# Counting the first expert's tokens on two engines with three PSUM banks, and transposing the first softmax one chunk of scores later

## The chip, the cores and the metric

The kernel runs on one core of one Trainium2 chip. Its time is the device time of one execution in microseconds (us). Before the change it is 1360.89 us, the median of three runs (1357.67 to 1362.44). The core has TensorE (PE in the profile; PEld are its weight loads), VectorE (DVE), ScalarE (ACT), GpSimd (POOL) and SyncE (SP), each with a queue of its own that it works off in order, and 16 DMA engines that all queues share.

## The reference

Attention between channels, then a mixture of eight experts. There are 4 batches of 5056 tokens with 256 channels, 20224 tokens in all.

```
qn = q / (norm(q, axis=1) + 1e-6);  kn = k / (norm(k, axis=1) + 1e-6)   # over the tokens
s  = kn^T @ qn / tau            # per batch: 256 x 256
a  = softmax(s)                 # over the last axis
x  = (v @ a)                    # 20224 x 256
logits = x @ w_gate             # 20224 x 8
# go through all (token, expert) pairs by falling logit; a token takes the first expert
# that still has room; each expert takes cap = 20224 / 8 = 2528 tokens
for e in range(8):
    out[mine[e]] = relu(x[mine[e]] @ w1[e]) @ w2[e]    # 256 -> 1024 -> 256
```

## The kernel before, in words

**Scores stage.** For each batch, five chunks of 1024 tokens (the last has 960 in 120 partitions) are loaded by SP as two halves with `k` and `q` side by side in a tile `ua`, of which there are four. TensorE adds `k^T q` into a PSUM bank (L239, 16 fp32 products per chunk); ScalarE squares the halves (L247) and VectorE sums the squares (L248) for the norms. After the fifth chunk four pairs of small products give the norms (L256), and a few operations make the scaling vectors (`lengths`).

The softmax of batch b runs on VectorE while TensorE does the scores of batch b+1: two small products spread the scaling (L281), VectorE makes the matrix `ac` (ending at L311), four transposes turn it (L319, `turned_a`), products with the gate weights follow (L328, `gates`), and ScalarE writes the result as `a` (L330, L331). With `a` a chunk of values can be multiplied (L197, `x_tiles`: 16 products, one value job) and its result `x` stored to DRAM by ScalarE's queue (L207). What stands where is given by tables: `LOADS` (which value chunk is loaded behind which chunk of scores), `JOBS` (which jobs stand behind which chunk: "x" a value job of batch 0, "l" a piece of the logits, L343) and `GATES_AT` (behind which chunk the transposes stand for batches 1 and 2; the gates stand one chunk later). Inside this stage a scheduler orders the instructions of an engine from the order in which they are written.

**Routing.** The thirteen value chunks left over (`TODO`) keep TensorE busy while VectorE routes the first expert. For each expert a search over thresholds (`route`: eight steps, each comparisons on VectorE, 20 products L495 and one L508 on TensorE) finds the expert's tokens. `compact` then turns the mask into an index list: for each of the 20 columns of 128 slots, TensorE multiplies (L704) into a PSUM tile `pi` that holds three columns, ScalarE counts with a sign function that accumulates (L709, one instruction and a read per column), and copies two more numbers out as `ext` (L712). With the counts of all columns VectorE computes the list `src` (L715 to L746). `pi` is one PSUM bank, so the products of the next three columns wait for the `ext` of the three before.

From here on a planner written in the kernel (class `Order`) sets the order: each stream of work names an engine and a cost, and the planner puts it between the main products when its modelled time has come. `compact` is such a stream.

**Experts.** GpSimd gathers an expert's tokens by `src` from DRAM (L937), TensorE transposes them (L964), ScalarE and VectorE split them into a high and a low part (`xH`, `xL`), and two layers follow (L999 with `hH`, `hL` of L1002 and L1007; L1030 with `y`), whose rows GpSimd scatters to the output (L1037). The weights of an expert are gathered by its number (L907) and split into `ua` in eight pieces (L916 on ScalarE, L919 on VectorE). The search for the next expert runs between these products.

## Time and profile before

| | us |
|---|---|
| median of three runs | 1360.89 (1357.67 to 1362.44) |
| profiled execution, its own time | 1353.34 |
| span of its instructions | 1351.6 |
| TensorE busy | 1306.5 (97%) |
| VectorE busy | 758.3 (56%) |
| ScalarE busy | 532.7 (39%) |
| GpSimd busy | 357.2 (26%) |

The scores stage ends near 210 us, the value chunks near 343 us, and the first products of an expert start at 352.4 us. A line of the profile such as `L704 PE MATMUL pi<-E_,G` is line 704 of the kernel, the engine, the operation, and the tiles written and read. In a row of the timeline the first number is the start and the second the time to the end of the last of the merged instructions; the bracket is the engine's idle time before it and what ended it.

### The profile page before, as it was taken

Reading aid. Unit: us, or ns where it says so; the run is one execution under the profiler, and the core shown is the slowest. Engines: PE = TensorE matmul, PEld = TensorE weight load, DVE = VectorE, ACT = ScalarE, POOL = GpSimd, SP = SyncE. Lnnn points to the kernel's source line nnn. Section 1 sums busy time; section 2 is a strip of 40 time slices with the busy share of each in tenths; the row PEclk is TensorE's granted clock in tenths of the full one; section 3 lists DMA queues with packets and bytes.
Section 4 is the critical chain, followed back from the end, with each engine's and each line's share of the span. In section 5 each row is a group of like instructions: output and inputs, shape, how many; then the busy total and the mean of one; then the engine's idle time right before and its main releaser. Section 6 shows DMA issues by size and latency. Waiting matters only on the chain.

```text
span 1351.6 us, 22840 instructions
## 1 busy us (share of the span) xinstructions
PE 1306.5 (97%) x9138; PEld 1154.2 (85%) x9138; DVE 758.3 (56%) x1890; ACT 532.7 (39%) x1210; POOL 357.2 (26%) x526
## 2 busy tenths in 40 slices
PE   8989999999599999999999999999999999999998
PEld 6878877887488888888889888989898998899898
DVE  6746395767478659668657666672334224233321
ACT  5545452236134334435325424344533334333321
POOL 0000010000322443334323423333334333434122
PEclk9989999999699999999999999999999999999999
DMA  8998974245312112112111311131122113111000
GB/s 288 385 345 316 325 237 176 94 136 196 98 31 87 51 59 94 44 44 101 47 33 44 112 33 40 44 104 44 51 70 85 36 48 108 51 44 57 16 32 31
DMA packets 53706, 143.13 MB, mean 106 GB/s; under 512 B 7776, under 2 KB 28640, under 8 KB 48992
## 3 DMA queue, kind: packets, MB, share of 16 engines
q1 hardware_dynamic: 14544, 62.40, 13.4%
q0 software_dynamic: 17664, 58.22, 13.2%
q10 hardware_dynamic: 21392, 21.06, 4.6%
q8 instruction: 71, 1.16, 0.4%
q14 instruction: 35, 0.29, 0.1%
HBM read 99.97 MB, written 41.68 MB: 105 GB/s over the span
## 4 chain that ended last, share of the span: by engine, by line
PE 71%; issue 12%; DVE 5%; POOL 5%; DMA 4%; ACT 1%; another core or an unknown queue 1%; SPq 0%; POOLq 0%; ACTq 0%
PE ph L999 25%; PE py L1030 24%; PE px L197 9%; PE s L239 7%; POOL out_dram L1037 3%; DMA x_d<-xs 2%; PE pc L495 2%; POOL xg L937 2%; DMA ua<-in_q_dram 2%; PE pt L964 1%; PE px L343 1%; PE pi L704 1%; DVE acc_q L248 1%; DVE ge L526 0%
## 5 line engine op out<-in xcount | busy, mean ns | idle before, releaser
L1030 PE MATMUL py<-ua,hH 128*128 128x256 f32 (+1 forms) x2560 | 468.1, 283 | 0.0
L999 PE MATMUL ph<-xH,ua 128*128 128x512 f32 (+3 forms) x1312 | 420.4, 393 | 9.4 <-issue 6.4
L1030 PEld LDWEIGHTS py<-ua,hH 128*128 128x128 f32 (+1 forms) x2560 | 390.3, 186 | 0.4
L1030 PE MATMUL py<-ua,hL 128*128 128x256 f32 (+1 forms) x1280 | 358.4, 280 | 0.0
L1007 DVE SCALAR_TENSOR_TENSOR hL<-ph,hH 128x512 fp32r<-128x512 f32 (+3 forms) x328 | 219.0, 669 | 178.7 <-ACT hH L1002 141.3
L1037 POOL DMA_INDIRECT out_dram<-y,idx x160 | 160.4, 1003 | 545.7 <-ACT y L1035 500.3
L999 PEld LDWEIGHTS ph<-xH,ua 128*128 128x128 f32 x1312 | 245.6, 190 | 59.8 <-issue 6.6
L1002 ACT ACTIVATE hH<-ph 128x512 fp32r<-128x512 f32 (+3 forms) x328 | 190.4, 583 | 247.3 <-PE ph L999 205.9
L999 PE MATMUL ph<-xL,ua 128*128 128x512 f32 (+3 forms) x656 | 256.9, 392 | 0.2 <-DVE xL L969 0.2
L1030 PEld LDWEIGHTS py<-ua,hL 128*128 128x128 f32 (+1 forms) x1280 | 238.6, 186 | 0.0
L1035 ACT ACTIVATE y<-py 128x256 f32<-128x256 f32 (+1 forms) x160 | 61.4, 384 | 337.6 <-PE py L1030 280.0
L937 POOL DMA_INDIRECT xg<-x_d,src x160 | 154.2, 964 | 119.0 <-issue 45.1
L239 PE MATMUL s<-ua 128*128 128x256 f32 (+1 forms) x640 | 146.4, 390 | 7.4 <-DMA ua<-in_q_dram 7.4
L239 PEld LDWEIGHTS s<-ua 128*128 128x128 f32 (+1 forms) x640 | 124.3, 196 | 27.4 <-issue 6.2
L999 PEld LDWEIGHTS ph<-xL,ua 128*128 128x128 f32 x656 | 125.0, 190 | 23.7 <-DVE xL L969 0.8
L969 DVE TENSOR_TENSOR xL<-pt,xH 128x512 fp32r<-128x512 f32 (+3 forms) x82 | 54.5, 665 | 125.6 <-ACT xH L966 125.0
L197 PE MATMUL px<-a,vr 128*128 128x256 f32 (+1 forms) x448 | 103.4, 385 | 0.9 <-ACT a L331 0.9
L247 ACT ACTIVATE sq<-ua 128x1024 f32<-128x1024 f32 (+1 forms) x72 | 75.8, 1056 | 58.4 <-DMA ua<-in_k_dram 24.5
L197 PEld LDWEIGHTS px<-a,vr 128*128 128x128 f32 x448 | 82.9, 190 | 12.3 <-ACT a L331 1.0
L201 ACT ACTIVATE xs<-px 128x512 f32<-128x512 f32 (+1 forms) x96 | 50.2, 527 | 91.5 <-PE px L197 88.0
L709 ACT ACTIVATE junk<-pi,rhalf 128x160 bf16<-128x160 f32 x160 | 61.8, 391 | 33.0 <-PE pi L704 27.2
L498 DVE TENSOR_TENSOR Dm<-pc,dmask 128x64 f32<-128x64 f32 (+3 forms) x63 | 12.7, 201 | 86.8 <-PE pc L495 56.9
(265 smaller groups left out, 1091.6 us busy)
## 6 DMA issues: line engine op xcount, KB each, us to landing
x_d<-xs ACTq DMA_DIRECT2D x19, 1024.0 KB, 4.6
ua<-in_k_dram SPq DMA_DIRECT2D x31, 512.0 KB, 5.9
ua<-in_q_dram SPq DMA_DIRECT2D x31, 512.0 KB, 7.2
vr<-in_vt_dram SPq DMA_DIRECT2D x14, 1024.0 KB, 10.6
ua<-in_vt_dram SPq DMA_DIRECT2D x4, 1024.0 KB, 5.2
ua<-in_k_dram SPq DMA_DIRECT2D x8, 480.0 KB, 6.7
ua<-in_q_dram SPq DMA_DIRECT2D x8, 480.0 KB, 8.8
xg<-x_d,src POOLq DMA_INDIRECT x160
```

The lines of the kernel that those rows point to most:

```text
L197: mm = PE.matmul(px[:, i * C:i * C + width], lhsT=vs[b, c][:, kb, t + i, :], rhs=a_f[b][:, kb, 0:width], start=(kb == 0), stop=(kb == 1))
L239: newest[0] = PE.matmul(sb[:, ib * C:(ib + 1) * C], lhsT=kt[:np_, t, ib * 128:(ib + 1) * 128], rhs=qt[:np_, t, :], start=(first and t == 0 ...
L247: S.activation(sq[:np_], t_[:np_], AF.Square)
L709: S.activation(junk, pi[:, i * W:i * W + COLS], AF.Sign, bias=rhalf[:, g0 + i:g0 + i + 1], scale=-1.0, accum_out=sgn[:, g0 + i:g0 + i + 1])
L937: queue.append(lambda i=i, col=col, n=n_in(col): P.indirect_dma_start(out=xg[:n, i, :], out_offset=None, in_=x_d, in_offset=bass.IndirectO ...
L969: V.tensor_tensor(xL[:, kb, 0:nt], pt[:, 0:nt], xH[:, kb, 0:nt].bitcast(F32), op=OP.subtract)
L999: PE.matmul(ph[:, 0:nt], lhsT=l[:, w], rhs=x_[:, kb, 0:nt], start=(i == 0), stop=(i == 5))
L1002: S.activation(hH[:, fb, 0:nt], ph[:, 0:nt], AF.Relu)
L1007: V.scalar_tensor_tensor(hL[:, fb, 0:nt], ph[:, 0:nt], 0.0, hH[:, fb, 0:nt].bitcast(F32), op0=OP.max, op1=OP.subtract)
L1030: PE.matmul(py[:n, 0:C], lhsT=l[:, fb, tk], rhs=w[:, d], start=(j == 0), stop=(j == 23))
L1035: S.activation(y[:n], py[:n, 0:C], AF.Copy)
L1037: sd = P.indirect_dma_start(out=out, out_offset=bass.IndirectOffsetOnAxis(ap=idx[:n, col:col + 1], axis=0), in_=y[:n], in_offset=None)
```

## The change

1. **The scores stage's tables.** `GATES_AT` puts the first transposes behind the fourth chunk of scores instead of the third, and the gates behind the fifth. The value jobs of batch 0 and the first pieces of the logits each move back one place. The softmax is written behind the jobs of chunk 0 instead of ahead of them.
2. **The first expert's `compact`** is cut into two streams: `by_act` tests the first 11 columns on ScalarE as before, out of two PSUM banks; `by_dve` tests the other 9 on VectorE with a comparison that accumulates, out of the bank that there was. VectorE then turns both counts into `at`. The other seven experts keep the old way. The two new banks come from a pool that is closed when the experts' pools open.
3. **The waits ahead of the experts' pools**: the loop that lets the planner run until the first expert's number and list are there stands before the pools are opened instead of behind.

```diff
+NACT = 11
-JOBS = {(1, 3): [("x", 0)], (1, 4): [("x", 1)], (2, 0): [("x", 2)], (2, 1): [("x", 3)], (2, 2): [("x", 4)],
-        (2, 4): [("l", 0)], (3, 0): [("l", 1)], (3, 1): [("l", 2)],
+JOBS = {(1, 4): [("x", 0)], (2, 0): [("x", 1)], (2, 1): [("x", 2)], (2, 2): [("x", 3)], (2, 3): [("x", 4)],
+        (3, 0): [("l", 0)], (3, 1): [("l", 1)], (3, 2): [("l", 2)],
         "tail": [("w", (1, 1)), ("l", 3), ("l", 4), ("l", 5), ("l", 6), ("l", 7)]}
-GATES_AT = (2, 3)
+GATES_AT = (3, 3)
...
-                put(0, soft)
+                todo[0].append(soft)
...
+    cctx = ExitStack()
+    two = [cctx.enter_context(tc.tile_pool(name="two", bufs=2, space=PSUM))]
...
+        def by_act():
+            todo = list(range(0, NACT, RB))
+            held = []
+            while todo or held:
+                while todo and len(held) < 2:
+                    g0 = todo.pop(0)
+                    n = min(RB, NACT - g0)
+                    pi = two[0].tile([128, 512], F32, name="pi")
+                    yield "P", n * 75
+                    tested(pi, g0, n)
+                    held.append((pi, g0, n))
+                pi, g0, n = held.pop(0)
+                for i in range(n):
+                    yield "A", 700
+                    junk = rtile("junk", dt=BF, bufs=2)
+                    S.activation(junk, pi[:, i * W:i * W + COLS], AF.Sign, bias=rhalf[:, g0 + i:g0 + i + 1], scale=-1.0,
+                                 accum_out=sgn[:, g0 + i:g0 + i + 1])
+                yield "A", 200
+                S.activation(ext[:, g0:g0 + n], pi[:, 0:n * W].rearrange("p (i w) -> p i w", w=W)[:, :, COLS:W], AF.Copy)
...
+        def by_dve():
+            num = rtile("num", (128, NCOL))
+            for g0 in range(NACT, NCOL, RB):
+                n = min(RB, NCOL - g0)
+                pi = ps_c.tile([128, 512], F32, name="pi")
+                yield "P", n * 75
+                tested(pi, g0, n)
+                for i in range(n):
+                    yield "V", 370
+                    junk = rtile("junkv", dt=BF, bufs=2)
+                    V.tensor_scalar(junk, pi[:, i * W:i * W + COLS], rhalf[:, g0 + i:g0 + i + 1], 0.0, op0=OP.is_lt,
+                                    op1=OP.add, accum_out=num[:, g0 + i:g0 + i + 1])
+                yield ve(2 * n, psum=True)
+                V.tensor_copy(ext[:, g0:g0 + n], pi[:, 0:n * W].rearrange("p (i w) -> p i w", w=W)[:, :, COLS:W])
+            yield ve(NCOL)
+            V.tensor_copy(at[:, NACT:NCOL], num[:, NACT:NCOL])
...
+        if p == 0:
+            o.add(by_act(), lambda: COMPACT_PRIO)
+            o.add(by_dve(), lambda: COMPACT_PRIO - 1)
...
+        o.until(("ei", 0))
+        settle()
+        o.until(("idx", 0))
         actx.close()
+        cctx.close()
...
-        o.until(("ei", 0))
-        settle()
-        o.until(("idx", 0))
```

Three places show how instructions move. Line numbers of the changed kernel are its own, a few above those of the profile (L320 is the old L319, L725 and L728 the old L709 and L712). First, TensorE from the first softmax's L281 to the second's; before:

```order
L281 MATMUL pc<-dq,ones_f 128x128 x2
L239 MATMUL s<-ua 128x256 x32
L319 MATMUL pm<-ident,ac 128x128 x4
L239 MATMUL s<-ua 128x256 x16
L328 MATMUL pm<-wg_t,aT 128x8 x4
L197 MATMUL px<-a_169,vr 128x264 x16
L239 MATMUL s<-ua 128x256 x16
L197 MATMUL px<-a_169,vr 128x264 x16
L256 MATMUL pc<-ones_f,acc_k 128x1 x2
L256 MATMUL pc<-ones_f,acc_q 128x1 x2
L239 MATMUL s<-ua 128x256 x16
L281 MATMUL pc<-dq,ones_f 128x128 x2
```

and now:

```order
L282 MATMUL pc<-dq,ones_f 128x128 x2
L240 MATMUL s<-ua 128x256 x48
L320 MATMUL pm<-ident,ac 128x128 x4
L240 MATMUL s<-ua 128x256 x16
L329 MATMUL pm<-wg_t,aT 128x8 x4
L257 MATMUL pc<-ones_f,acc_k 128x1 x2
L257 MATMUL pc<-ones_f,acc_q 128x1 x2
L198 MATMUL px<-a_169,vr 128x264 x16
L240 MATMUL s<-ua 128x256 x16
L198 MATMUL px<-a_169,vr 128x264 x16
L282 MATMUL pc<-dq,ones_f 128x128 x2
```

Three chunks of scores instead of two now stand between L281 and the transposes, and no value job stands before the batch's last chunk any more; from one L281 to the next the amount of work is the same.

Second, ScalarE behind the store of a value chunk (L207, now L208) during the first expert's counting; before:

```order
L207 DMA x_d<-xs 1024x1x256
L712 ACTIVATE ext<-pi 128x6
L201 ACTIVATE xs<-px 128x2x256
L916 ACTIVATE ua<-ub 128x512
L709 ACTIVATE junk,sgn<-pi,rhalf 128x160 x2
L201 ACTIVATE xs<-px 128x2x256
L916 ACTIVATE ua<-ub 128x512
L709 ACTIVATE junk,sgn<-pi,rhalf 128x160
L201 ACTIVATE xs<-px 128x2x256
L916 ACTIVATE ua<-ub 128x512
L712 ACTIVATE ext<-pi 128x6
```

and now:

```order
L208 DMA x_d<-xs 1024x1x256
L725 ACTIVATE junk,sgn<-pi,rhalf 128x160 x2
L202 ACTIVATE xs<-px 128x2x256
L971 ACTIVATE ua<-ub 128x512
L725 ACTIVATE junk,sgn<-pi,rhalf 128x160
L728 ACTIVATE ext<-pi 128x6
L202 ACTIVATE xs<-px 128x2x256
L971 ACTIVATE ua<-ub 128x512
L725 ACTIVATE junk,sgn<-pi,rhalf 128x160 x2
```

Between the store and the next `ext` but one there stood three evictions (L201) and three weight pieces (L916) before; now one of each stands before the second set's `ext`.

Third, VectorE at the same time, with the next expert's first steps (`m`, `t`, `khi`, `eq`) between its tests; now:

```order
L741 TENSOR_SCALAR junkv,num<-pi,rhalf 128x160
L454 TENSOR_REDUCE m<-L_146 128x160
L741 TENSOR_SCALAR junkv,num<-pi,rhalf 128x160
L457 TENSOR_SCALAR t_2230<-m 128x160
L741 TENSOR_SCALAR junkv,num<-pi,rhalf 128x160
L460 TENSOR_SCALAR tie<-t_2230 128x160
L744 COPY ext<-pi 128x6
L462 TENSOR_TENSOR t_2230<-t_2230,tie 128x160
L465 TENSOR_SCALAR khi<-t_2230 128x160
```

All L741 and L744 rows are new on VectorE; the others stood here before in the same order.

More of the change, by code (lines that the diff above doesn't have):

```diff
@@ L698, in compact, with tested @@
         ext = rtile("ext", (128, NCOL, 2))
-        for g0 in range(0, NCOL, RB):
+        at = rtile("at", (128, NCOL), I32)
+        ended = []
+        def tested(pi, g0, n):
+            for i in range(n):
+                PE.matmul(pi[:, i * W:(i + 1) * W], lhsT=G[:, (g0 + i) * 128:(g0 + i + 1) * 128], rhs=E_,
+                          start=True, stop=True)
+        def by_act():
[17 more added lines that the diff above has]
+                S.activation(ext[:, g0:g0 + n], pi[:, 0:n * W].rearrange("p (i w) -> p i w", w=W)[:, :, COLS:W], AF.Copy)
+            ended.append(1)
@@ new lines, in by_dve @@
+        def by_dve():
[5 more added lines that the diff above has]
+                tested(pi, g0, n)
+                for i in range(n):
+                    yield "V", 370
[6 more added lines that the diff above has]
+            V.tensor_copy(at[:, NACT:NCOL], num[:, NACT:NCOL])
+            ended.append(1)
@@ L700, in compact @@
+        if p == 0:
+            o.add(by_act(), lambda: COMPACT_PRIO)
+            o.add(by_dve(), lambda: COMPACT_PRIO - 1)
+            while len(ended) < 2:
+                yield "W", 0
+            yield ve(NCOL)
+            V.tensor_scalar(at[:, 0:NACT], sgn[:, 0:NACT], 0.5, COLS / 2.0, op0=OP.mult, op1=OP.add)
+        for g0 in range(0, NCOL if p else 0, RB):
             n = min(RB, NCOL - g0)
@@ L702, in compact @@
             yield "P", n * 75
+            tested(pi, g0, n)
             for i in range(n):
-                PE.matmul(pi[:, i * W:(i + 1) * W], lhsT=G[:, (g0 + i) * 128:(g0 + i + 1) * 128], rhs=E_,
-                          start=True, stop=True)
-            for i in range(n):
-                yield "A", 600 if p else 900
+                yield "A", 600
                 junk = rtile("junk", dt=BF, bufs=2)
@@ L712, in compact @@
             S.activation(ext[:, g0:g0 + n], pi[:, 0:n * W].rearrange("p (i w) -> p i w", w=W)[:, :, COLS:W], AF.Copy)
-        at = rtile("at", (128, NCOL), I32)
-        yield ve(NCOL)
-        V.tensor_scalar(at, sgn, 0.5, COLS / 2.0, op0=OP.mult, op1=OP.add)
+        if p:
+            yield ve(NCOL)
+            V.tensor_scalar(at, sgn, 0.5, COLS / 2.0, op0=OP.mult, op1=OP.add)
         k1 = rtile("k1", (128, NCOL), I32)
```

## The prediction

> **What bounds the kernel now.** I read the page's busy shares, then TensorE's waits from 0 to 365 us, where the edit lies. The busy line and four of the waits:
>
> ```profile
> PE 1306.5 (97%) x9138; PEld 1154.2 (85%) x9138; DVE 758.3 (56%) x1890; ACT 532.7 (39%) x1210; POOL 357.2 (26%) x526
> PE pm L319 <- DVE ac L311: 4.1, 1, 4.1
> PE pi L704 <- ACT ext L712: 2.6, 2, 2.4
> PE pc L281 <- DVE dq L280: 2.3, 2, 1.5
> PE ph L999 <- issue: 6.4, 1, 6.4
> ```
>
> TensorE is busy in 97% of the span, so only its idle time, its slow time and work taken off it can move the end. (A row of waits gives the sum in us, how often, the longest.) Two of these waits belong to steps that the change touches in the scores stage: 4.1 us for the first softmax's `ac`, 2.3 us for `dq`. The third, 2.6 us for `ext`, belongs to the first expert's counting. The fourth, at the first expert's first products, has no named cause.
>
> TensorE's own timeline over the first wait, batch 1's scores onward (start, duration, instruction, records, wait in brackets; two records to an fp32 product, so x32 is one chunk):
>
> ```profile
> 60.28 7.14 PE L239 MATMUL s<-ua 128*128 128x256 f32 x32 [0.62 <-DMA ua<-in_q_dram]
> 71.57 1.08 PE L319 MATMUL pm<-ident,ac 128*128 128x128 f32 x4 [4.14 <-DVE ac L311]
> 72.44 9.48 PE L239 MATMUL s<-ua 128*128 128x256 f32 x32
> 81.76 0.95 PE L328 MATMUL pm<-wg_t,aT 128*128 128x8 f32 x8
> 83.66 7.39 PE L197 MATMUL px<-a,vr 128*128 128x264 f32 x32 [0.95 <-ACT a L331]
> 90.89 7.07 PE L239 MATMUL s<-ua 120*128 120x256 f32 x32
> 97.80 7.29 PE L197 MATMUL px<-a,vr 128*128 128x264 f32 x32
> 104.92 0.50 PE L256 MATMUL pc<-ones_f,acc_k 128*128 128x1 f32 x4
> 105.73 7.15 PE L239 MATMUL s<-ua 128*128 128x256 f32 x32
> 114.36 0.46 PE L281 MATMUL pc<-dq,ones_f 128*128 128x128 f32 x2 [1.47 <-DVE dq L280]
> 115.59 0.49 PE L281 MATMUL pc<-dq,ones_f 128*128 128x128 f32 x2 [0.78 <-DVE dq L280]
> 115.92 7.29 PE L197 MATMUL px<-a,vr 128*128 128x264 f32 x32
> ```
>
> One undisturbed chunk of scores takes 97.80 - 90.89 = 6.91 us, one value chunk 104.92 - 97.80 = 7.12, the norms 105.73 - 104.92 = 0.81. The chunk at 72.44 lasts 81.76 - 72.44 = 9.32, which is 2.4 too long. The granted clock says why (a stretch: its length; busy time of TensorE, weight loads, VectorE, ScalarE, GpSimd; then the clock, the DMA engines' busy share and GB/s):
>
> ```profile
> 72.00:78.00 6.00, 6.00 (x19) 4.93 (x18) 4.31 (x4) 2.49 (x3) 0.00 (x0) 0.56 1.02 237
> 310.00:320.00 10.00, 7.64 (x38) 6.53 (x37) 8.35 (x10) 6.89 (x21) 0.00 (x0) 1.00 0.53 187
> ```
>
> After the 4.14 us wait the clock is 0.56 on average from 72 to 78. A 2.36 us wait at 314.47 left it at 1.00. And the DMA engines are full at 72 to 78 (1.02) with only 237 GB/s moved. That matters next.
>
> **First part: the transposes one chunk later.** On TensorE the order after the first softmax's `rq` becomes: chunks 1, 2 and 3 of scores, the transposes (L319), chunk 4, the gates' products (L328), the norms, value job 0, the next batch's chunk 0, value job 1, then that batch's L281. Before it was: chunks 1, 2, L319, chunk 3, L328, value 0, chunk 4, value 1, norms, chunk 0, L281. The work up to L281's end is the same, so the two orders can be laid against each other from the end of chunk 2 (60.28 + 7.14 = 67.42) to L281's end (115.92, where value job 2 starts): 48.50 us before.
>
> Chunk 3 now starts at 67.42, where the transposes waited; `ac` is written by 71.57, and L319 is not reached before 74.8. So the 4.14 us wait has 6.91 us of products over it and goes, and so does the slow clock after it. What is late next is the loads. Issue and time to landing of the second operand of chunk 3's first half and of chunk 4's two halves, in that order (a half needs both operands, and this is the later one):
>
> ```profile
> 56.65 1.07 SPq L234 DMA_DIRECT2D ua<-in_q_dram  x1
> 64.43 0.41 SPq L234 DMA_DIRECT2D ua<-in_q_dram  x1
> 68.67 0.41 SPq L234 DMA_DIRECT2D ua<-in_q_dram  x1
> ua<-in_q_dram SPq DMA_DIRECT2D x1, 512.0 KB, 11.1
> ua<-in_q_dram SPq DMA_DIRECT2D x1, 480.0 KB, 14.5
> ua<-in_q_dram SPq DMA_DIRECT2D x1, 480.0 KB, 15.1
> ```
>
> Chunk 3's first half lands at 56.65 + 11.1 = 67.75: a wait of about 0.4, then 67.8 + 6.9 = 74.7. Its second half is needed 3.46 (half a chunk) later, and I take it as there. The transposes took 72.44 - 71.57 = 0.87 at the slow clock, so about 0.5 now: 75.2. Chunk 4's first half lands only at 64.43 + 14.5 = 78.93, its second at 68.67 + 15.1 = 83.77. These issues wait for the buffers of chunk 2, whose place is unchanged, and the DMA engines were full already, so I take the landings as they stand. Before, chunk 4 ran at 90.89, so this lateness cost nothing. Now TensorE waits 75.2 to 79.0 = 3.8 us, runs half a chunk (3.46) to 82.5, waits to 83.85 = 1.3, and ends chunk 4 at 87.3. Then:
>
> gates 0.9 -> 88.2; norms 0.8 -> 89.0, which cover the 0.95 us wait for `a`; value 0 7.1 -> 96.1; chunk 0 6.9 -> 103.0; value 1 7.1 -> 110.1; L281 0.5 -> 110.6. The waits of 1.47 and 0.78 for `dq` go too, because the norms now end 21 us ahead of L281 instead of 7.
>
> 115.92 - 110.6 = **5.3 us earlier**. Bounds: if chunk 4's loads came in time, 3.8 + 1.3 more would go: 10.4; if the first half also ran at half clock (rival 1), 2.2 less: 3.1.
>
> Later in the scores stage every load has its value chunk between two chunks of scores as before. SP's two moved loads of `vr` go one place later in a queue whose other loads keep their order; their buffers are read a chunk later as well, so they cost nothing while the value jobs cover them (their price if not: one 1 MB load, rival 3).
>
> **Second part: counting shared.** TensorE still makes 20 tests, and ScalarE's 11 and VectorE's 9 now sit in three banks. Rows of the stretch (timeline rows; the last two are groups: busy us, mean ns, idle):
>
> ```profile
> 301.67 2.79 PE L197 MATMUL px<-a,vr 128*128 128x256 f32 x12
> 304.30 0.37 PE L704 MATMUL pi<-E__97,G 128*128 128x162 bf16 x3
> 304.51 4.95 PE L197 MATMUL px<-a,vr 128*128 128x256 f32 x22
> 316.83 0.37 PE L704 MATMUL pi<-E__97,G 128*128 128x162 bf16 x3 [2.36 <-ACT ext L712]
> 321.39 0.75 PE L495 MATMUL pc<-oh,ge 128*128 128x64 bf16 x20
> 324.18 0.41 PE L508 MATMUL pc<-Ex,ones_q 128*128 128x128 f32 x1
> 312.46 0.60 ACT L201 ACTIVATE xs<-px 128x512 f32<-128x512 f32 x1 [3.31 <-DMA x_d<-xs]
> 316.57 0.20 ACT L712 ACTIVATE ext<-pi 128x6 f32<-128x6 f32 x1
> 305.73 2.10 DVE L451 TENSOR_REDUCE m<-L 128x160 f32<-128x1120 f32 x1
> L692 DVE TENSOR_TENSOR E__97<-pc,sc_a 128x160 bf16<-128x160 f32 x1 | 0.3, 310 | 0.0
> L519 DVE DVE_READ_ACCUMULATOR hit<-mxs 128x1 f32 x4 | 0.3, 83 | 0.0
> ```
>
> Removed: the wait of 2.36 at 316.83 and one of 0.26. TensorE also issues one search step of the next expert less before the last value product: an L495 set and an L508. Rows give 0.75 and 0.41 with overlap; I take 0.8. That step isn't saved but moved behind; the wait for the first gather has room for it.
>
> Added: waits at three tests. A set of three tests costs 304.51 - 304.30 = 0.21. Call ScalarE's sets a0 to a3, VectorE's d0 to d2; d1 reuses d0's bank, a2 a0's, a3 a1's. Counting from 301.67 with 0.445 per value product:
> - d1 is reached at 309.15. VectorE begins d0's tests at 305.73, and L451 (2.10) stands among them. One test is not in the trace; I bound it by 0.31 (L692, the same 160 elements out of PSUM) and 0.62 (a second pass) and take 0.31 + 0.08 for the accumulator's read = 0.39. Three tests, L451, two small operations near 0.28 and the read-out end near 309.8: 0.65 wait.
> - a3 is reached at 313.1 and needs a1's `ext`. ScalarE is held until 312.46 by the store as before (3.31). Before, three evictions, three weight pieces and three tests stood between 312.46 and the next `ext` at 316.57; a1 now needs one of each, (316.77 - 312.46 - 0.2)/3 + 0.2 = 1.6: `ext` at 314.1, wait 1.0.
> - d2 is reached at 319.2. VectorE had 1.65 us idle from 310 to 320; d1's three tests and read-out (about 1.4) fill it, so the read-out comes near 319.9: 0.7 wait. The first search step then starts about 0.3 late.
>
> New waits 0.65 + 1.0 + 0.7 + 0.3 = 2.65, removed 2.6 + 0.8 = 3.4: **0.7 us earlier**. Bounds: no new wait, 3.4 earlier; each of the three as long as the 2.36, 3 x 2.36 - 3.4 = 3.7 later.
>
> The earlier index list doesn't start the first gather earlier by itself. Rows around that gather and the first products behind it:
>
> ```profile
> 343.48 0.37 ACTq L207 DMA_DIRECT2D x_d<-xs  x1
> 363.66 0.38 ACT L1002 ACTIVATE hH<-ph 128x256 fp32r<-128x256 f32 x1 [10.64 <-remote]
> 346.75 0.95 POOL L937 DMA_INDIRECT xg<-x_d,src  x1 [43.88 <-DVE Dm L498]
> 360.81 0.23 DVE L498 TENSOR_TENSOR Dm<-pc,dmask 128x64 f32<-128x64 f32 x1 [7.32 <-remote]
> ```
>
> `src` used to be ready just before the gather; but the gather reads what the last store wrote. It goes out at 343.48 and the gather follows 3.3 us later. That distance stays. The reordered waits ahead of the new pools cost nothing: the gather's wait covers them.
>
> **The sum.** 5.3 + 0.7 = 6.0 us against the profiled execution (span 1351.6, its own time 1353.34): 1347.3. That execution is 7.55 us below the median of the runs, 1360.89, so the same step from the median gives 1354.9, and I say **1355.0**. Experts 1 to 7 get their search steps a little later; their index lists have hundreds of products to spare, so nothing for them.
>
> **Rivals.** About 0.3%, 4.1 us, is what a measurement here can tell from no change: 1356.8 and 1365.0 are the marks.
>
> 1. The half clock comes back behind the load wait. For it: 3.8 idle us is near the 4.14 that halved the clock; against: 2.36 didn't, and the transposes and the half chunk of products stand close around this wait. Price: the first half of chunk 4 at half speed takes 3.46 longer, of which 1.3 was waiting anyway: 2.2. Time 1357.2. [...]
> 2. No new wait: chunk 4's loads land in time, or the new tests never wait. For it: `ext` banks are three instead of one. Price 2.65 (the tests) to 5.1 (the loads) better: 1351.
> 3. The loads set the pace: what TensorE gains it waits out at the next batch's loads. For it: the DMA share of 1.02. Against: the load wait in TensorE's rows above is 0.62, and from batch 2 on a value chunk of 7.12 lies between two chunks of scores again. Price: the 5.3 is gone, 0.7 stays: 1360.2.
> 4. Slower: the hole at the first expert grows. There VectorE waited 7.32 and ScalarE 10.64 us for a TensorE that had issued its products long before; a search step's L495 set stands inside these products. In the new order the set stands three products later, and one more search step is still to come. If one more set falls into the hole, it costs up to another 10.64, and it decides as soon as it exceeds the 6.0 gained: 1355.0 + 10.6 = 1365.6.
>
> **Chances.** Forecast (1352.5 to 1357) 0.40; rival 1 0.27; rival 2 0.13; rival 3 0.10; rival 4 0.10. Faster than 1356.8: four fifths of the forecast, 0.32, two fifths of rival 1, 0.11, all of rival 2: together 0.55 with rounding. Slower than 1365.0: six tenths of rival 4 and a little noise, 0.07. Between: 0.38. The range runs from rival 2 to most of rival 4: 1350 to 1363, which leaves out the worst of rival 4 and a gain of over 10.9; the forecast's own is 1352.5 to 1357.
>
> **What would show it.** Right: no wait at L319; a wait of 3 to 4 us at chunk 4's first products, a shorter one at its second half; the second L281's end near 110.6; waits of `pi` tests of 2 to 3 us in sum, at ScalarE's last set above all; the first gather 5 to 7 us earlier. Rival 1 shows as a clock near 0.5 behind the load wait, rival 3 as load waits between 110 and 200 us, rival 4 as a longer wait of ScalarE's first `hH`. The forecast is wrong if chunk 4's loads land at another time than before, or if the first `hH` moves against the first gather by more than 3 us.

## The result: slower by 0.74%

| | before | changed |
|---|---|---|
| median of the runs, us | 1359.05 (1355.75 to 1362.44, 6 runs) | 1368.65 (1366.71 to 1372.23, 6 runs) |
| ratio to before | | 1.0074, 95% interval 1.0059 to 1.0089 |
| profiled execution: span, own time | 1351.6, 1353.34 | 1364.9, 1366.71 |

1355.0 was predicted, 6 us faster, with a range up to 1363; it came out 9.6 us slower. The edited stages are not where the time went. Up to the first gather the changed kernel is ahead by most of what was forecast. First TensorE around the transposes, in the timeline of the changed kernel (start, duration, instruction, records, wait in brackets; L240, L320, L329, L198, L282 are the old L239, L319, L328, L197, L281):

```profile
68.14 7.14 PE L240 MATMUL s<-ua 128*128 128x256 f32 x32 [0.48 <-DMA ua<-in_q_dram]
75.12 0.60 PE L320 MATMUL pm<-ident,ac 128*128 128x128 f32 x4
79.08 8.83 PE L240 MATMUL s<-ua 120*128 120x256 f32 x32 [3.36 <-DMA ua<-in_q_dram]
87.75 0.96 PE L329 MATMUL pm<-wg_t,aT 128*128 128x8 f32 x8
110.91 0.61 PE L282 MATMUL pc<-dq,ones_f 128*128 128x128 f32 x4
125.97 2.05 PE L198 MATMUL px<-a,vr 128*128 128x264 f32 x8 [2.21 <-ACT xs L202]
```

The wait for `ac` (4.14 us before) is gone, chunk 4 waits for its loads until 79.08, and L282 starts at 110.91. A new wait of 2.21 us stands behind it. The norms of the last batch, by the timeline of the kernel before:

```profile
209.24 0.50 PE L256 MATMUL pc<-ones_f,acc_k 128*128 128x1 f32 x4
```

and of the changed one:

```profile
206.32 0.50 PE L257 MATMUL pc<-ones_f,acc_k 128*128 128x1 f32 x4
```

2.9 us ahead there. Then the first gather, and the first expert's first holes, in the changed kernel:

```profile
342.15 1.18 POOL L992 DMA_INDIRECT xg<-x_d,src  x1 [42.19 <-DVE low L568]
355.63 0.38 PE L1054 MATMUL ph<-xH,ua 128*128 128x256 f32 x1 [1.60 <-DVE hL L1062]
359.86 0.58 PE L1054 MATMUL ph<-xH,ua 128*128 128x256 f32 x1 [3.26 <-DVE hL L1062]
362.84 0.58 PE L1054 MATMUL ph<-xH,ua 128*128 128x256 f32 x1 [1.34 <-DVE hL L1062]
```

The gather goes out at 342.15; before it was 346.75: 4.6 ahead. So 4.6 + 13.3 = 18 us of span are lost behind it, among the experts, where no instruction of the forecast had a price. TensorE is busy for longer there, with the same number of instructions. The groups of the page that carry it, before:

```profile
L1030 PE MATMUL py<-ua,hH 128*128 128x256 f32 (+1 forms) x2560 | 468.1, 283 | 0.0
L999 PE MATMUL ph<-xH,ua 128*128 128x512 f32 (+3 forms) x1312 | 420.4, 393 | 9.4 <-issue 6.4
L1030 PE MATMUL py<-ua,hL 128*128 128x256 f32 (+1 forms) x1280 | 358.4, 280 | 0.0
L999 PE MATMUL ph<-xL,ua 128*128 128x512 f32 (+3 forms) x656 | 256.9, 392 | 0.2 <-DVE xL L969 0.2
L239 PE MATMUL s<-ua 128*128 128x256 f32 (+1 forms) x640 | 146.4, 390 | 7.4 <-DMA ua<-in_q_dram 7.4
```

and changed, with the busy line:

```profile
PE 1320.8 (97%) x9138; PEld 1166.7 (85%) x9138; DVE 763.6 (56%) x1912; ACT 528.0 (39%) x1189; POOL 361.7 (26%) x526
...
L1085 PE MATMUL py<-ua,hH 128*128 128x256 f32 (+1 forms) x2560 | 478.7, 286 | 2.1 <-issue 2.1
L1054 PE MATMUL ph<-xH,ua 128*128 128x512 f32 (+3 forms) x1312 | 422.8, 395 | 7.8 <-DVE hL L1062 7.3
L1085 PE MATMUL py<-ua,hL 128*128 128x256 f32 (+1 forms) x1280 | 363.6, 284 | 0.0
L1054 PE MATMUL ph<-xL,ua 128*128 128x512 f32 (+3 forms) x656 | 259.2, 395 | 0.2 <-DVE xL L1024 0.2
L240 PE MATMUL s<-ua 128*128 128x256 f32 (+1 forms) x640 | 145.6, 388 | 11.5 <-DMA ua<-in_q_dram 11.5
```

Busy time grew by 14.3 us with 9138 matmuls in both. A py product lasts 3 to 4 ns longer in the mean, a ph product 2 to 3, a score product not at all. Since matmuls overlap (before, a py product of `hH` lasts 283 ns in the mean and the next one starts 116.8 ns after it), the distance from the start of one to the start of the next says more. Two equal stretches of py products late in the kernel, the first and the last row of seven groups of three products, before:

```profile
1197.02 0.40 PE L1030 MATMUL py<-ua,hH 128*128 128x256 f32 x2
...
1199.49 0.38 PE L999 MATMUL ph<-xH,ua 128*128 128x480 f32 x1
```

and changed:

```profile
1207.82 0.41 PE L1085 MATMUL py<-ua,hH 128*128 128x256 f32 x2
...
1210.34 0.38 PE L1054 MATMUL ph<-xH,ua 128*128 128x480 f32 x1
```

21 products take 2.47 us before, 2.52 now: 117.6 and 120.0 ns each, with nothing waited for. Over the whole trace (all pairs of products of one line that follow each other directly, those over 1.4 times the median left out) the mean distance of py went from 116.8 to 119.7 ns and of ph from 229.8 to 231.0. Priced over all 3687 and 1847 such pairs of the changed kernel, that is 10.7 + 2.2 = 12.9 us. The score products (216.5 ns) and value products (221 ns) kept theirs. These two numbers, the "pace" from here on, are what the experiments read. The py number is the steadier one: in the seven traces here whose tiles lie, within 256 bytes, as in the kernel before, it is 116.8 to 116.9, while ph is 228.3 to 230.5. So the 2.2 us of ph are less sure than the 10.7.

Two more losses show in this execution. Length, busy time of TensorE, weight loads, VectorE, ScalarE and GpSimd, then the granted clock, DMA share and GB/s of four stretches of time, before:

```profile
473.00:480.00 7.00, 5.99 (x68) 5.92 (x67) 1.48 (x5) 1.68 (x5) 3.95 (x6) 1.00 0.32 97
480.00:483.50 3.50, 2.26 (x20) 2.06 (x18) 3.10 (x7) 2.24 (x5) 2.04 (x3) 1.00 0.14 42
770.00:776.70 6.70, 6.26 (x46) 4.67 (x45) 2.34 (x7) 1.50 (x3) 4.10 (x6) 1.00 0.58 202
776.70:780.20 3.50, 2.99 (x13) 2.12 (x12) 3.14 (x10) 1.87 (x4) 0.00 (x0) 1.00 0.00 0
```

and changed:

```profile
473.00:480.00 7.00, 4.36 (x31) 3.84 (x30) 0.58 (x3) 1.31 (x4) 3.54 (x6) 0.98 0.28 86
480.00:483.50 3.50, 3.50 (x19) 3.50 (x19) 3.43 (x10) 1.78 (x4) 2.15 (x4) 0.54 0.13 42
770.00:776.70 6.70, 4.35 (x37) 3.20 (x36) 2.56 (x15) 0.60 (x1) 4.37 (x6) 1.00 0.63 230
776.70:780.20 3.50, 3.50 (x9) 2.53 (x9) 2.71 (x12) 1.68 (x3) 0.00 (x0) 0.51 0.00 0
```

In the first and third of these stretches TensorE is now idle for 2.6 and 2.4 us, the second time ahead of a step of the next expert's search, and each time it then runs at half clock for some 3.4 us.

Laid side by side at equal py products (start in the changed kernel less start before, the first product counted as 0), the whole account is: -4.9 us at 0, -3.8 at 372, -0.6 at 408 (the first hole and half clock, 3.2), +0.4 at 480, -1.8 at 1360 (holes that only the kernel before had), -0.8 at 1434, +2.8 at 1440 (the second hole and half clock, 3.6), then steadily up to +13.15 at 3760.

### The profile page after: what moved, and what is told of

It is laid out like the page before. It is cut to its first block, busy times and chain, and to the rows that moved or that the text cites. A ratio compares the mean times of both kernels' runs of the same rounds, so it can differ in the third digit from the quotient of the medians.

```text
span 1364.9 us, 22830 instructions
## 1 busy us (share of the span) xinstructions
PE 1320.8 (97%) x9138; PEld 1166.7 (85%) x9138; DVE 763.6 (56%) x1912; ACT 528.0 (39%) x1189; POOL 361.7 (26%) x526
## 4 chain that ended last, share of the span: by engine, by line
PE 72%; issue 12%; DMA 5%; POOL 5%; DVE 3%; ACT 1%; another core or an unknown queue 1%; SPq 0%; POOLq 0%; ACTq 0%
PE ph L1054 25%; PE py L1085 25%; PE px L198 8%; PE s L240 7%; DMA ua<-in_q_dram 3%; POOL out_dram L1092 3%; PE pc L498 3%; DMA x_d<-xs 2%; POOL xg L992 2%; PE pt L1019 1%; PE px L344 1%; PE pi L707 1%; PE pc L511 0%; ACT hH L1057 0%
## 5 line engine op out<-in xcount | busy, mean ns | idle before, releaser
L1085 PE MATMUL py<-ua,hH 128*128 128x256 f32 (+1 forms) x2560 | 478.7, 286 | 2.1 <-issue 2.1
L1085 PEld LDWEIGHTS py<-ua,hH 128*128 128x128 f32 (+1 forms) x2560 | 395.2, 188 | 2.0 <-issue 1.5
L1085 PE MATMUL py<-ua,hL 128*128 128x256 f32 (+1 forms) x1280 | 363.6, 284 | 0.0
L992 POOL DMA_INDIRECT xg<-x_d,src x160 | 157.9, 987 | 115.4 <-issue 53.4
L240 PE MATMUL s<-ua 128*128 128x256 f32 (+1 forms) x640 | 145.6, 388 | 11.5 <-DMA ua<-in_q_dram 11.5
L240 PEld LDWEIGHTS s<-ua 128*128 128x128 f32 (+1 forms) x640 | 123.4, 194 | 31.8 <-issue 14.8
L198 PE MATMUL px<-a,vr 128*128 128x256 f32 (+1 forms) x448 | 103.7, 385 | 2.3 <-ACT xs L202 2.2
L198 PEld LDWEIGHTS px<-a,vr 128*128 128x128 f32 x448 | 82.8, 190 | 14.4 <-ACT xs L202 3.1
L764 ACT ACTIVATE junk<-pi,rhalf 128x160 bf16<-128x160 f32 x140 | 54.2, 392 | 24.9 <-PE pi L707 22.8
```

The costliest lines, as they stand in the source:

```text
L198: mm = PE.matmul(px[:, i * C:i * C + width], lhsT=vs[b, c][:, kb, t + i, :], rhs=a_f[b][:, kb, 0:width], start=(kb == 0), stop=(kb == 1))
L240: newest[0] = PE.matmul(sb[:, ib * C:(ib + 1) * C], lhsT=kt[:np_, t, ib * 128:(ib + 1) * 128], rhs=qt[:np_, t, :], start=(first and t == 0 ...
L764: S.activation(junk, pi[:, i * W:i * W + COLS], AF.Sign, bias=rhalf[:, g0 + i:g0 + i + 1], scale=-1.0, accum_out=sgn[:, g0 + i:g0 + i + 1])
L992: queue.append(lambda i=i, col=col, n=n_in(col): P.indirect_dma_start(out=xg[:n, i, :], out_offset=None, in_=x_d, in_offset=bass.IndirectO ...
L1085: PE.matmul(py[:n, 0:C], lhsT=l[:, fb, tk], rhs=w[:, d], start=(j == 0), stop=(j == 23))
```

## The experiments

What is there that no instruction row shows? The changed kernel allocates two more tiles, `num` (80 bytes per partition, in a slot of 96) and `junkv` (two of 320), in the pool `rt` that stays open. 96 + 640 = 736: the experts' pool behind it, with `xg`, `xH`, `xL`, `hH`, `hL`, `y`, begins 736 bytes later in each partition. `hH` moved from byte 149728 to 150464. Every other tile that a TensorE product reads, the weights' `ua` and `ub` among them, and all PSUM banks of the experts, stayed. Theory "places": that alone slows the products. Rival "order": they are slower because the search stands elsewhere among them (of its products of L495, now L498, the 300th has 91 ph and py products ahead of it instead of 2, the 560th 1001 instead of 987; the expectation of run 5 numbers them 360 and 660).

The experiments ran in four groups of four, each on one device together with runs of the kernel before. That has a median of 1359.6 us beside the first group and of 1335.7, 1334.7 and 1334.1 beside the others ("the first" and "the later devices" below; the device of the result above is not on record, and by its 1359.05 us it is counted with the first). Each ratio is to before in its own group.

### 1. The kernel before, its experts' tiles 736 bytes later

```diff
+        rtile("pad", (128, 184))
         ffx = ctx.enter_context(tc.tile_pool(name="ffx", bufs=2))
```

> The kernel before, with an unused tile of 736 bytes per partition put in front of the experts' tiles (xg, xH, xL, hH, hL, y), so that these lie where the changed kernel has them; every engine's instructions stay as they were, and nothing is left out. Between the two profiled kernels the mean distance from one py product to the next went from 116.8 to 119.7 ns (x3687) and from one ph product to the next from 229.8 to 231.0 ns (x1847), while the products of scores (216 ns) and values (216 ns) and the counts of the search (25 ns) kept theirs. Theory 'places': the change's new tiles num and junkv moved the experts' tiles by 736 bytes in SBUF, and that alone slows each product: py near 119.7 ns, ph near 231, time longer by 3687 x 2.9 + 1847 x 1.2 = 12.9 us, a ratio near 1.009. Rival 'order': the pace follows how the search and the gathers stand among the products in the changed kernel; then this kernel has 116.8 and 229.8 ns and the time of before, ratio 1.000.

Measured: 1369.69 us, ratio 1.0062 (1.0045 to 1.0078). Pace 119.7 and 230.3 ns. The page's groups:

```profile
L1030 PE MATMUL py<-ua,hH 128*128 128x256 f32 (+1 forms) x2560 | 478.5, 285 | 0.0
L1030 PE MATMUL py<-ua,hL 128*128 128x256 f32 (+1 forms) x1280 | 362.0, 283 | 0.0
```

The same instructions in the same order, with an unused tile ahead of six others, lose as much as the whole change does: 10.1 us against 9.6. "Order" falls as the cause of the pace.

### 2. The changed kernel, its experts' tiles where they were

```diff
+    tally = cctx.enter_context(tc.tile_pool(name="cnt", bufs=1))
-            num = rtile("num", (128, NCOL))
+            num = tally.tile([128, NCOL], F32, name="num")
-                    junk = rtile("junkv", dt=BF, bufs=2)
+                    junk = tally.tile([128, COLS], BF, name="junkv", bufs=2)
```

> The changed kernel, with num and junkv taken from a pool of their own that is closed before the experts' tiles are made, so that these lie at the very addresses of the kernel before; order and work as in the changed kernel. Theory 'places': py back to 116.8 ns, ph to 229.8, the time 12.9 us below the changed kernel's 1368.65, near 1355.8, a ratio to before near 0.997. Rival 'order': py stays at 119.7 ns and the time at 1368, ratio 1.007.

Measured: 1357.69 us, ratio 0.9983 (0.9969 to 0.9997), pace 116.8 and 230.5:

```profile
L1086 PE MATMUL py<-ua,hH 128*128 128x256 f32 (+1 forms) x2560 | 469.1, 283 | 1.1 <-issue 0.9
L1086 PE MATMUL py<-ua,hL 128*128 128x256 f32 (+1 forms) x1280 | 360.2, 281 | 0.0
```

11 us come back by moving two scratch tiles into a pool that closes. The change without its side effect is faster, here by 2.3 us (0.4 to 4.2).

### 3 and 4. Pads of 32 and 64 bytes

> The kernel before with an unused tile of 32 bytes in front of the experts' tiles, nothing left out. Before, hH begins at byte 149728 of a partition, 32 beyond a multiple of 64, as the weights' ua does (39456); in the changed kernel at 150464, a multiple of 64. If 'places' holds and what counts is the place within 64 bytes, this has py near 119.7 ns and a time near 1372; if a coarser place counts, py stays at 116.8 ns and the time near 1359; by 'order' too.

> The kernel before with an unused tile of 64 bytes in front of the experts' tiles, nothing left out. If 'places' holds with the place within 64 bytes, py stays at 116.8 ns and the time near 1359; if a coarser place counts, py may go anywhere between 116.8 and 119.7 ns or beyond; by 'order' nothing moves, as for the pad of 32.

Measured, one time each: with 32 bytes 1359.34 us, pace 117.0 and 229.9; with 64 bytes 1360.65 us, pace 119.5 and 225.8. So the place within 64 bytes isn't it, and the two kinds of products don't move together: with 64 bytes py is as slow as in the changed kernel, by 3687 x 2.7 = 10.0 us, while ph is 4 ns faster than before, 1847 x 4 = 7.4 us. Together that is 2.6 us slower; the one time is 1.0 above before, too few runs to tell.

### 5 and 6. The two halves of the change

5 is the scores part alone (`JOBS`, `GATES_AT`, `soft`), 6 the counting part alone, with `num` and `junkv` in the pool that closes.

> The kernel before with the first half of the change alone: the tables JOBS and GATES_AT and the place of soft (scores). The experts' tiles lie where they lay, and among the experts' products the search stands as before (its 360th count behind 2 main products, its 660th behind 987; in the changed kernel behind 91 and 1001). Theory 'search': the two halves of the clock that the changed kernel has at 478 and 775 us come from where the count half has put the search's steps; so this keeps the gain of the forecast's first part, 5.3 us on paper and 4.6 to 4.9 in the changed kernel's trace at the first gather: a time near 1359.6 - 4.8 = 1354.8, a ratio near 0.9965. Rival 'eaten': a lead at the experts' start is lost behind it by whatever order, since the search of the next expert is what the second expert waits for; then the time is 1357 to 1360 and the ratio 0.998 to 1.000.

> The kernel before with the second half of the change alone: the first expert's counts shared by ScalarE and VectorE with three banks, and the wait for the first index list ahead of the experts' pools; num and junkv in a pool that is closed before the experts' tiles are made, so that these lie where they lay before. By the forecast's second part: 0.7 us less, near 1358.9, ratio 0.9995. Theory 'search': the next experts' search steps now stand 14 to 120 main products later, the holes of 2 to 2.4 us ahead of a search step near 475 and 772 us come back, each with the clock halved behind it: 2 x (2 + 1.7) us lost against 0.7 gained, some of it caught up with by 1060 us: near 1361 to 1364, ratio 1.001 to 1.003. Theory 'eaten': as the kernel before, ratio 0.999 to 1.001.

Measured: the scores part 1332.90 against 1335.73, ratio 0.9981 (0.9966 to 0.9995); the counting part 1332.96, ratio 0.9984 (0.9971 to 0.9996). So 2.5 us (0.7 to 4.5) for a forecast of 5.3, and 2.1 (0.5 to 3.9) for one of 0.7. The theory "search" falls, at least on this device: run 6 has the search where the changed kernel has it, and its trace (mean granted clock 0.994) shows neither of the halves of the clock near 478 and 775. For run 5 the time is the one that "eaten" named, but in its trace not in that way: against the trace of run 12 below, run 5 is 2.9 us ahead at the values, 1.1 at the first py product and still 1.1 at the end, and run 6 is 1.7 ahead at the first py product and 2.9 at the end. In this pair of traces what was lost was lost across the counting, ahead of the experts; behind their start nothing was eaten. With both halves (run 11, by the same trace) the 3.1 us at the values become 5.5 at the first py product, as if the counting part let the scores part's lead through.

That is argued from single traces, and those scatter. In the ten traces of the old order here the first gather goes out between 345.2 and 352.0 us (median 348.3), in the six of the whole new order between 342.2 and 346.8 (median 343.4); run 5 has 348.6 and run 6 347.1. So the lead of the whole change at the first gather is there, 4.9 us by the medians. Where run 5 lost its part is not shown.

### 7 and 8. A place for each expert

```diff
-        hH = ffx.tile([128, 8, 512], F32R, name="hH")
+        hH, hL = (ffx.tile([128, 8 * 512 + 128], F32R, name=nm)[:, p * 8:p * 8 + 4096].rearrange(
+            "p (f n) -> p f n", f=8) for nm in ("hH", "hL"))
```

(and `xH`, `xL` in the same way; `p * 16` in run 8.)

> The kernel before with hH, hL, xH and xL cut out of tiles 512 bytes longer, from byte 32p on for expert p, so that each expert runs its products from another place within 256 bytes; order and work as before. With the whole set of tiles moved by 0, 32, 64 and 736 bytes the mean distance of py products was 116.8, 117.0, 119.5 and 119.7 ns and that of ph products 229.8, 229.9, 225.8 and 230.3. If the place of hH and hL within 128 or 256 bytes sets the pace of py, and that of xH and xL the pace of ph, the experts show at least two levels each, about 117 and 119.6 ns for py, 226 and 230 for ph, that follow p with a period of 4 or 8. If something else that moved with them counts (xg or y), all experts show one level.

> As the one before, but from byte 64p on (0 to 448 for the eight experts). The place within 64 bytes stays one; if a place within 128 bytes counts, the experts alternate between two levels; within 256, with a period of 4; within 512, of 8. If nothing moved here counts, one level.

Measured, one time each, 1336.70 and 1337.04 us. The mean distance in ns within one execution, by expert (here pairs over 1.15 times the median are left out); "place" is the byte within 256 at which `hH`, `hL`, `xH` and `xL` begin:

| expert | 0 | 1 | 2 | 3 | 4 | 5 | 6 | 7 |
|---|---|---|---|---|---|---|---|---|
| run 7: place | 224 | 0 | 32 | 64 | 96 | 128 | 160 | 192 |
| py | 117.3 | 117.0 | 119.4 | 118.2 | 115.7 | 118.2 | 119.2 | 119.8 |
| ph | | | 225.3 | 229.6 | 227.1 | 230.4 | 229.1 | 230.5 |
| run 8: place | 224 | 32 | 96 | 160 | 224 | 32 | 96 | 160 |
| py | 117.4 | 119.3 | 116.0 | 118.9 | 117.3 | 119.6 | 115.9 | 119.3 |
| ph | | | 227.0 | 229.4 | 230.0 | 225.0 | 226.6 | 229.1 |

(ph of experts 0 and 1 is left blank: their smaller chunks make another mean.) The levels repeat with 256 bytes in run 8, expert for expert. The changed kernel's tiles begin at 192, the worst place for py in the table; the kernel before had 224. The best for py is 96, for ph 32. Not every difference between experts is one of place: in the kernel before, with all eight at 224, py goes in 116.5 to 117.7 ns in experts 0 to 4 and in 116.0 in 5 to 7. Why is open.

### 9, 10 and 11. Places chosen from the table

9 is the kernel before and 10 the changed kernel of run 2, both with `hH`, `hL` at 96 and `xH`, `xL` at 32; 11 is the changed kernel with a pad of 32 bytes more, so that 736 becomes 768 = 3 x 256.

```diff
+        hH, hL = (ffx.tile([128, 8 * 512 + 64], F32R, name=nm)[:, 32:32 + 4096].rearrange("p (f n) -> p f n", f=8)
+                  for nm in ("hH", "hL"))
...
+            xH, xL = (ffx.tile([128, 2 * 512 + 64], F32R, name=nm)[:, 16:16 + 1024].rearrange("p (f n) -> p f n", f=2)
+                      for nm in ("xH", "xL"))
```

> The kernel before, order and work as they were, with hH and hL begun at byte 96 and xH and xL at byte 32 within 256 bytes (all four at 224 before). In the two runs with a place for each expert, py went in 115.7 to 116.0 ns where hH lay at 96 (three experts; 116.8 to 117.4 at 224), ph in 225.0 ns where xH lay at 32 (expert 5, by 64; 230.0 at 224, expert 4). Theory 'places', with a period of 256 bytes: 3687 x 0.9 + 1847 x 4 = 3.3 + 7.4 = 10.7 us less than before on the same chip, a ratio near 0.992. Rival 'no period': what counts is more than the place within 256 bytes, and the experts' levels were their own; then py near 117, ph near 229, ratio 0.998 to 1.002.

> The changed kernel with num and junkv in the pool that is closed early, and with the places of the run above (hH, hL at 96, xH, xL at 32 within 256 bytes). Theory 'places': the 0.9983 of the changed kernel with its tiles where they lay, less 10.7 us: a ratio near 0.990 to before. Rival 'no period': 0.998.

> The changed kernel with an unused tile of 32 bytes behind num and junkv, nothing else, so that the experts' tiles lie 768 = 3 x 256 bytes from where they lay before instead of 736. Theory 'places' with a period of 256 bytes: py back from 119.7 to 116.8 ns, a ratio to before near 0.998 instead of the changed kernel's 1.0074. Rival 'no period': py stays near 119 ns or goes elsewhere, ratio 1.004 to 1.008.

| | us | ratio to before | py, ph ns |
|---|---|---|---|
| 9: before, places chosen | 1324.41 | 0.9927 (0.9911 to 0.9943) | 115.7, 224.2 |
| 10: changed, places chosen | 1317.69 | 0.9879 (0.9862 to 0.9895) | 115.6, 224.6 |
| 11: changed, 32 bytes more | 1328.98 | 0.9965 (0.9948 to 0.9982) | 116.9, 228.3 |

The groups of run 10:

```profile
L1086 PE MATMUL py<-ua,hH 128*128 128x256 f32 (+1 forms) x2560 | 462.4, 282 | 0.0
L1055 PE MATMUL ph<-xH,ua 128*128 128x512 f32 (+3 forms) x1312 | 410.8, 387 | 0.7 <-DVE hL L1063 0.7
```

All three came out by "places" with a period of 256 bytes, run 10 a little better than it; 32 unused bytes turn the changed kernel from 0.74% slower (0.51% in run 16, on a later device) into 0.35% faster. Run 10 is faster than both kernels, by 1.2% against before.

### 12. The kernel before once more

> The kernel before once more, unchanged, for a trace of this chip beside the others: py 116.8 ns and ph near 229 to 230 ns by either theory; the half-clock windows between 60 and 380 us, and those by chance behind 470 us, are what may differ from its first trace.

One time, 1336.4 us, pace 116.9 and 228.5. It gives a trace of the kernel before from the later devices. Against it, run 11 is 5.5 us ahead at the first py product, 4.9 to 7.0 until 590 us, 5.5 to 9.6 until 1010 and 6.45 from 1040 to the end. So a lead of the size of the forecast's 6.0 is carried to the end of the kernel once the tiles lie well. Its size isn't fixed by one pair of traces: run 9, the old order on the same device, is 2.5 us ahead of run 12 at the first py product. By all runs of run 11 the gain is 4.7 us (2.4 to 6.9). Between 473 and 480 us and between 770 and 776.7 us the changed order has no hole on a later device (run 15, the kernel of run 2 again):

```profile
473.00:480.00 7.00, 7.00 (x73) 6.28 (x71) 3.71 (x13) 1.85 (x4) 2.85 (x5) 1.00 0.12 40
770.00:776.70 6.70, 6.70 (x49) 5.33 (x48) 3.97 (x14) 2.47 (x5) 4.72 (x5) 1.00 0.24 73
```

### 13 to 16. Which tile, against what, and both kernels on one device

13 is the kernel before with only `hH` and `hL` moved (to 96). 14 is run 9 with 32 unused bytes ahead of everything, `ua` at 64 within 256 instead of 32, `hH`, `hL`, `xH`, `xL` still at 96 and 32:

```diff
+    const.tile([128, 8], F32, name="padc")
     ident = const.tile([128, 128], F32, name="ident")
```

15 is run 2 again, 16 the changed kernel itself.

> The kernel before with hH and hL begun at byte 96 within 256 and xH and xL left at 224. With hH at 96 and xH at 32 together py went in 115.72 ns and ph in 224.2 to 224.6. If hH and hL set py's pace alone and xH and xL that of ph: py 115.7, ph 228.5 to 229.8 as in the kernel before. If the x tiles' place had a part in py or that of h in ph: something between.

> The kernel before with hH and hL at byte 96 and xH and xL at byte 32 within 256, as in the run that was 0.9927 of before, but with 32 unused bytes ahead of everything, so that the weights' ua lies at 64 within 256 bytes instead of 32. If the places of h and x count by themselves: py 115.7 and ph 224.2 to 224.6 again. If they count against the weights' place, this is as h at 64 and x at 0 with the weights at 32: py 118.2 to 119.8 and ph near 230.

> The changed kernel with the experts' tiles where they lay before, once more. The order alone: a ratio to before of 0.9983 on the first chip, 0.9965 with the pad of 32 bytes on the second. If the gain hangs on the chip's half-clock windows behind 470 us, it is near 0.998 where a trace has them and near 0.9955 where not.

> The changed kernel as it is, beside the run above on the same chip. If the 736 bytes are all that stands between them, py is 119.7 ns against 116.8 and the difference 3687 x 2.9 + 1847 x 1.0 = 12.5 us by the products' distances, 10 to 13 by the times; a ratio to before of 1.005 to 1.0075.

| | us | ratio to before | py, ph ns |
|---|---|---|---|
| 13: only hH, hL moved | 1334.01 (one time) | | 116.3, 228.3 |
| 14: weights moved | 1341.70 (one time) | | 118.2, 228.8 |
| 15: changed, tiles where they were | 1330.13 | 0.9965 (0.9950 to 0.9980) | 116.9, 228.4 |
| 16: changed | 1341.65 | 1.0051 (1.0038 to 1.0064) | 119.7, 229.7 |

In run 13 ph kept its pace and py gained; it gained less than in run 9 (115.9 for the first five experts, 116.9 for the last three; in run 9 115.7 and 115.8). Runs 9 and 13 differ in the place of `xH` and `xL` alone, so something besides the place of `hH` has a small part in py. Run 14's groups:

```profile
L1031 PE MATMUL py<-ua,hH 128*128 128x256 f32 (+1 forms) x2560 | 473.3, 285 | 0.0
L1000 PE MATMUL ph<-xH,ua 128*128 128x512 f32 (+3 forms) x1312 | 417.1, 392 | 0.4 <-DVE hL L1008 0.4
```

The 32 bytes move every tile, and the offsets bring the four back to their places, so that of the operands of these products only the weights have moved. py went to 118.2 and ph of the later experts to 230: what run 7 shows for `hH` at 64 (118.2), the same distance from `ua`. So the weights' place counts as well, and the numbers fit a place that counts not by itself but against that of the product's other operand. This was tried at one distance only; for the others it is not shown. In these terms py is best with `hH` 64 bytes beyond `ua` within 256 (115.7), was at 192 (116.8), and is slowest at 160 (119.8), where the change put it; ph is best at 0.

Runs 15 and 16 settle the account on one device: 11.5 us between the changed kernel and the same with its tiles where they were, 12.9 by the pace (3687 x 2.87 + 1847 x 1.23). The order of the change by itself is faster, by 3.9 us of the medians, 4.7 by the ratio (2.7 to 6.7).

## Why the prediction was wrong, step by step

- **"Experts 1 to 7 get their search steps a little later ... so nothing for them."** This is the sentence that failed, for a reason that it didn't name. It priced what was moved in time among the experts, and nothing that was moved in memory. Two scratch tiles of the counting moved the tiles that 5808 products read, and each of these became 1 to 3 ns slower: 12.9 us by the pace, 10.1 us by the times of run 1, 11.5 by those of runs 15 and 16. No rival had it. For the profiled executions the forecast was 1347.3 and 1366.71 came. Of these 19.4 us 12.9 are the pace, 6.8 the two holes with their half clock (3.2 and 3.6 of the account above), 1.4 the lead missing at the first gather; 1.7 were caught up elsewhere, by difference.
- **First part, 5.3 us.** Mechanism right, size half. Forecast and measured: L320 reached near 74.8, 75.12; chunk 4's first half at 79.0, 79.08, its wait 3.8, 3.36; gates at 87.3, 87.75; L282's end 110.6, 111.35 (the start of the next scores), so 4.6 earlier than before instead of 5.3. Rival 1 came along with it: behind this wait the granted clock was 0.50 for 3.41 us, and the chunk's 8.83 us, with these in it, took the place of the forecast's second wait of 1.3, so it cost 0.5 and not 2.2. The stretch at that clock:

```profile
80.42:83.83 3.41, 3.41 (x9) 2.71 (x9) 2.42 (x3) 1.40 (x2) 0.00 (x0) 0.50 0.99 281
```

  What the step lacked is the 2.21 us at 123.76. ScalarE shows why:

```profile
121.07 0.66 ACT L202 ACTIVATE xs<-px 128x264 f32<-128x264 f32 x2
124.58 1.06 ACT L248 ACTIVATE sq<-ua 128x1024 f32<-128x1024 f32 x1 [2.86 <-DVE acc_k L249]
125.55 0.65 ACT L202 ACTIVATE xs<-px 128x264 f32<-128x264 f32 x2
```

  `xs` stands behind a square whose buffer VectorE had not summed yet. The work up to L282 was laid out without ScalarE's queue behind it. In the six other traces with the new tables this wait is 0.29 to 2.34 us long and the one for the loads 3.96 to 5.17. 4.6 less 2.2 leaves 2.4; 2.9 is there at the last norms, and 2.5 in run 5's time.
- **Second part, 0.7 us.** Right in kind, too small. A test on VectorE takes 0.38 us and the read of its accumulator 0.08 (forecast 0.31 + 0.08). Of the three waits forecast, 0.65 + 1.0 + 0.7, only one came, at ScalarE's last set, where the longest was forecast: 1.50 us.

```profile
311.17 0.30 PE L707 MATMUL pi<-E__97,G 128*128 128x162 bf16 x2 [1.50 <-ACT ext L728]
```

  and the tests on VectorE, shortest, median and longest in ns:

```profile
L741 DVE TENSOR_SCALAR_CACHE_REDUCE junkv<-pi,rhalf x9: 376/379/395, 302.7 to 320.4; 128x160 bf16<-128x160 f32 x9
```

  The lead grew from 2.9 to 4.6 across the counting: 1.7; run 6 has 2.1. The sum of both parts, 6.0, held better than its terms: 4.6 at the first gather in the changed kernel's trace, 5.5 at the first py product in run 11's.
- **The distance from the last store to the first gather, 3.3.** Right: the store goes out at 338.89, the gather at 342.15.
- **Rival 4, the hole at the first expert.** At the ph products it shrank: 1.60 + 3.26 + 1.34 = 6.2 us against 6.41 + 1.21 before. The first `hH` comes 12.6 us behind the first gather instead of 16.9. That move of 4.3 us is one of the signs that the prediction named for being wrong (more than 3), but towards the faster side:

```profile
345.21 0.34 PE L1019 MATMUL pt<-identr,xg 128*128 128x128 f32 x1 [5.13 <-DMA xg<-x_d,src]
354.73 0.38 ACT L1057 ACTIVATE hH<-ph 128x256 fp32r<-128x256 f32 x1 [6.08 <-PE ph L1054]
```

  Little of it was a gain: the lead is 4.4 us at the first ph product and 4.9 at the first py product.
- **Still open.** Why the two holes near 475 and 772 us, each with the clock halved behind it, stand in both traces of the new order from the first device (the changed kernel's and run 2's) and in none from the later ones. The half clock near 780 was in run 3 too, in the old order. The smaller gain of the order there (2.3 us, against 4.7 by the ratio in runs 11 and 15 on the later devices) fits this, but no run took the holes away on the first device.

## What to carry to other kernels

The two new tiles here moved the six behind them by 736 bytes, and 5808 products became slower (py from 116.8 to 119.7 ns, ph from 229.8 to 231.0). Compare the byte places of the operands of the busiest products before and after an edit, as one compares the order; where they changed, read the distance from product to product in a stretch without waits before looking for a lost wait. Put scratch tiles of one stage in a pool that closes before the next one's tiles are made (run 2: 11 us came back); and when a kernel is 97% TensorE, as this one is, try a trace with a different place for each expert (or layer): here runs 7 and 8 found places that were worth 0.7% (run 9).

## What the runs showed of the hardware that was not expected

- The pace of the fp32r products of 256 and 512 columns here depends on where their two operands lie in a partition, by run 14, at the one distance it tried, against each other, within 256 bytes, in steps of 32: 115.7 to 119.8 ns for py, 225.0 to 230.5 for ph, 3.5% and 2.4%. The best distance isn't the same for both: 64 bytes for py (115.7), 0 for ph (225.0). py has the hidden layer as its stationary and the weights as its moving operand, in ph the weights are stationary (`lhsT` of L1030 and L999). Whether another engine slows these products no run here tests. Why the places count, and whether other types and sizes show it, no run here tells.
- Waits and the granted clock: in the kernel before, a wait of 2.36 us at 314.47 left the clock at 1.00, while the 4.14 us that ended at 71.57 came with 0.50 for 6.83 us, from 70.49 on. In the changed kernel the 3.36 us that ended at 79.08 were followed by 0.50 for 3.41 us; but so were the 2.35 us at 773.99, in a stretch with 2.4 us idle in 6.7. And one and the same wait, that for `ext` in the old counting, went both ways: behind 2.77 us in run 5 the clock was 0.50, behind 3.42 us in run 14 it was 1.00.

```profile
316.99 0.37 PE L704 MATMUL pi<-E__97,G 128*128 128x162 bf16 x3 [2.77 <-ACT ext L712]
318.10:321.50 3.40, 3.40 (x9) 2.66 (x8) 3.37 (x6) 1.96 (x6) 0.00 (x0) 0.50 0.54 188
319.56 0.37 PE L705 MATMUL pi<-E__98,G 128*128 128x162 bf16 x3 [3.42 <-ACT ext L713]
319.20:325.00 5.80, 5.31 (x43) 4.61 (x43) 5.62 (x9) 4.92 (x15) 0.00 (x0) 1.00 0.49 167
```

  So in these traces the length of a wait alone does not decide, and what else does is open.
